# One load of r for a whole batch, six tokens to a partition, in a fused RWKV and token-mixing kernel

## The chip, the cores and the metric

The kernel runs on one core of one Trainium2 chip. The metric is the device time of one execution in microseconds (us); lower is better. The engines named below are TensorE (PE; PEld is its weight load), VectorE (DVE), ScalarE (ACT), GpSimd (POOL) and SyncE (SP), which here only issues DMAs.

## The reference

Two layers in sequence, for 4 batches, 8 heads, 768 tokens and 48 channels a head, all float32. The first is a linear attention with a state that decays per channel:

```python
for t in range(S):
    kt, vt, rt = (k[:, :, t], v[:, :, t], r[:, :, t])
    cur = np.einsum('bhd,bhe->bhde', u[None] * kt, vt)
    y[:, :, t] = np.einsum('bhd,bhde->bhe', rt, state + cur)
    state = w[None, :, :, None] * state + np.einsum('bhd,bhe->bhde', kt, vt)
```

Its output, with the heads side by side, is x (768 tokens by 384 channels for a batch). The second layer mixes tokens and channels:

```python
theta = x @ w_theta
zr, zi = x * np.cos(theta), x * np.sin(theta)
y = np.einsum('ts,bsd->btd', w_tok_r, zr) + np.einsum('ts,bsd->btd', w_tok_i, zi)
u = x + y
out = u + np.maximum(u @ w_ch, 0.0)
```

## The kernel before

**Tiling.** A batch's 768 tokens are six chunks of 128, worked on as three pairs of chunks; `g` counts the pairs over all batches (0 to 11). For a pair, `front` loads k, r and v, multiplies k and r by powers of w (`decay`, giving the bf16 tiles Kw and Rw), transposes both with TensorE (`flip`: one matmul against the identity for each block of 128 x 128, all into one PSUM bank, then one copy out by ACT or DVE, giving KT and RT), and makes the scores (KT against RT), which DVE multiplies with a mask into mAT. PD is the product of RT and KT for the diagonal term with u; `diag` and `yd` bring that to the output. `outer` makes a pair's contribution to the state, which F, T, N and the copies Sb and Sd carry from pair to pair in order. `states`, `outputs` and `bonus` add up the output of the pair in PSUM, and it is copied to x. Then x is transposed (xT), theta is a matmul, ACT takes cosine and sine of it (trig), and DVE makes z = x times trig. `mixing` multiplies z with the token weights WrT and WiT, which are themselves transposed once at the beginning from loads that GpSimd casts to bf16 (`cast`, `weights`). For an output chunk the mixing has three parts, one for each pair of z. Then comes the channel matmul with Wch, a maximum with zero, a sum and the store.

**Two layouts of tokens.** In the first seven pairs (`PAIRS`) k, v and r are loaded with two neighbouring tokens of a head on one partition, so that a run in memory is 2 x 48 floats, 384 bytes; r is loaded that way in all twelve pairs. In the others k and v have one token on a partition, 192 bytes. A transpose of a paired tile comes out with the even tokens in one block and the odd ones in the next; the copy out of PSUM puts them in order, by reading the two blocks in turn (the argument `paired` of `flip`).

**Powers.** `rpow` and `kpow` hold the powers of w for the two tokens on a partition; ACT makes them with one exponential for each of the two, from the logarithm of w and the column of `tok_f` that holds a token's distance from the middle of the pair.

**Buffers.** Sixteen load buffers (`Ls`, 128 x 768 float32, called ld in the profile) are given to the loads in turn. There are two Rw, four Kw, four RT and three KT, and eight PSUM banks.

**Order.** Every piece of work is a task in `Plan`. `ORDER` is one list of all tasks, written out beforehand; each engine runs its tasks in that order, and waits on semaphores for what a task reads or overwrites. `WAYS` says which engine does a task that several could do (copies out of PSUM, decay products, casts), `BANKS` gives the PSUM banks, `AFTER` adds waits between tasks that would otherwise run at the same time, and `IDLE` places filler matmuls on a tile of zeros (`unread`, line 293), whose result nobody reads. A load stands in SP's list, so a load that has to wait for its buffer also holds up what SP issues after it: other loads, transposes by DMA (line 510) and the stores.

**Lines.** 293 filler, 389 the logarithm, 399 the powers, 442 and 448 loads, 462 casting loads, 493 transposes, 503 and 504 their copies out by ACT and DVE, 554 and 556 decay products, 605 scores, 614 mAT, 621 PD, 638 and 643 the diagonal, 647 yd, 671 outer, 692 to 695 and 705 Sd, 719 F, 723 T, 726 and 727 N, 747 states, 760 outputs, 776 bonus, 784 and 786 x, 835 theta, 842 and 846 trig, 850 z, 901 mixing, 919 its sum, 929 the channel matmul, 956 to 964 the output.

Of the kernel before, what the change touches and what calls it, by code (L numbers as in the profile page):

```python
# [30 lines left out]
WARM, WARM_NS = (4, 6), (855, 1280)  # L31
NBANKS = 8
# [44 lines left out]
]  # L77
# [101 lines left out]
def kernel(  # L179
# [16 lines left out]
    C = 128  # L196
# [18 lines left out]
    def ring(n, shape, dt, nm):  # L215
        return [sb.tile(shape, dt, name=f"{nm}{i}") for i in range(n)]
# [81 lines left out]
    def setup():  # L298
# [93 lines left out]
        for i, (dst, nm, j, col) in enumerate((  # L392
# [3 lines left out]
            if dst is None:  # L396
                continue
# [623 lines left out]
```

## Time and profile before

| | |
|---|---|
| median of 3 runs | 136.62 us (136.30 to 137.31) |
| the profiled execution | 136.61 us, span 134.8 us |
| granted TensorE clock | 0.997 |
| PE busy | 127.9 us, 95% |
| DVE busy | 106.1 us, 79% |
| ACT busy | 81.0 us, 60% |
| POOL busy | 68.8 us, 51% |
| DMA | 25.47 MB in 67199 packets, 61801 of them under 512 bytes |

The span runs from the first instruction to the last; the time of an execution holds 1.8 us more around it. A line of a group names the source line, the engine, the operation and the tiles it writes and reads, then the shapes, the number of instructions, their busy time together, the mean of one in ns, and behind the second bar how long the engine was idle just before them and what ended that. A line of a timeline starts with the start and the duration in us. A line of the chain of work has start, duration, engine and line. A line of a table of stretches has the stretch, its length, and for each engine the busy us and the number of instructions; then the granted clock, the busy share of the DMA engines (above 1 where transfers overlap in the records) and GB/s.

### The profile page before, as it was taken

Reading aid. Unit: us, or ns where it says so; the run is one execution under the profiler, and the core shown is the slowest. Engines: PE = TensorE matmul, PEld = TensorE weight load, DVE = VectorE, ACT = ScalarE, POOL = GpSimd, SP = SyncE. Lnnn points to the kernel's source line nnn. Section 1 sums busy time; section 2 is a strip of 40 time slices with the busy share of each in tenths; the row PEclk is TensorE's granted clock in tenths of the full one; section 3 lists DMA queues with packets and bytes.
Section 4 is the critical chain, followed back from the end, with each engine's and each line's share of the span. In section 5 each row is a group of like instructions: output and inputs, shape, how many; then the busy total and the mean of one; then the engine's idle time right before and its main releaser. Section 6 shows DMA issues by size and latency. Waiting matters only on the chain.

```text
span 134.8 us, 4625 instructions
## 1 busy us (share of the span) xinstructions
PE 127.9 (95%) x1943; PEld 85.8 (64%) x1943; DVE 106.1 (79%) x201; ACT 81.0 (60%) x157; POOL 68.8 (51%) x76
## 2 busy tenths in 40 slices
PE   6999998899999999999999999899999999999970
PEld 1346666765776775876676776566667757667840
DVE  5099988687998999889798878799899997351370
ACT  3478696598968596684965153863731758900220
POOL 6003789295160456827326989664056955370220
PEclk9999999999999999999999999999999999999998
DMA  3999999999999955797999999979899950326344
GB/s 92 265 269 261 143 204 197 255 258 234 242 277 236 261 138 74 144 209 139 281 180 234 171 189 253 163 134 309 196 302 198 103 116 8 117 79 198 78 177 173
DMA packets 67199, 25.47 MB, mean 189 GB/s; under 512 B 61801, under 2 KB 67178, under 8 KB 67178
## 3 DMA queue, kind: packets, MB, share of 16 engines
q1 hardware_dynamic: 64744, 22.23, 76.3%
q0 software_dynamic: 2432, 2.95, 13.4%
q8 instruction: 15, 0.25, 0.8%
q14 instruction: 6, 0.05, 0.1%
q10 hardware_dynamic: 2, 0.00, 0.0%
HBM read 20.06 MB, written 4.72 MB: 184 GB/s over the span
## 4 chain that ended last, share of the span: by engine, by line
PE 78%; DVE 7%; DMA 5%; ACT 2%; POOL 2%; issue 2%; DVEq 0%; POOLq 0%; ACTq 0%
PE bank L901 31%; PE bank L493 11%; PE bank L835 8%; PE bank L929 7%; DMA uu_all<-uu_all 5%; PE bank L605 4%; PE bank L876 3%; PE bank L671 3%; PE bank L760 2%; PE bank L293 2%; DVE Rw L554 2%; PE bank L747 2%; PE bank L776 1%; PE bank L812 1%; PE bank L638 1%
## 5 line engine op out<-in xcount | busy, mean ns | idle before, releaser
L901 PE MATMUL bank<-z,WrT 128*128 128x384 bf16 x132 | 43.0, 326 | 0.0
L901 PE MATMUL bank<-z,WiT 128*128 128x384 bf16 x132 | 42.9, 326 | 0.0
L959 POOL TENSOR_TENSOR fin_all<-fin_all,uu_all 128x384 f32<-128x384 f32 x20 | 19.5, 992 | 22.7 <-ACT fin_all L956 8.7
L647 POOL TENSOR_TENSOR yd<-dg,vb 128x768 bf16<-128x768 f32 x10 | 14.7, 1471 | 11.8 <-DVE PD L621 5.1
L614 DVE TENSOR_TENSOR mAT<-bank,mask 128x512 bf16<-128x512 f32 x28 | 18.4, 682 | 0.3 <-PE bank L605 0.2
L901 PEld LDWEIGHTS <-WrT 128*128 128x128 bf16 x132 | 12.9, 98 | 7.7 <-issue 0.3
L956 ACT ACTIVATE fin_all<-bank 128x384 f32<-128x384 f32 x20 | 9.7, 494 | 12.9 <-issue 8.5
L901 PEld LDWEIGHTS <-WiT 128*128 128x128 bf16 x132 | 12.9, 98 | 7.1
L919 DVE TENSOR_TENSOR uu_all<-bank,x 128x384 bf16<-128x384 f32 x22 | 11.7, 553 | 5.3 <-PE bank L901 5.1
L842 ACT ACTIVATE trig<-bank,pi 128x384 f16<-128x384 f32 x24 | 13.4, 582 | 3.2 <-PE bank L835 3.2
L835 PE MATMUL bank<-Wth,xT 128*128 128x384 bf16 x72 | 14.3, 326 | 0.0
L850 DVE TENSOR_TENSOR z<-x,trig 128x1536 bf16<-128x1536 bf16 x12 | 11.4, 952 | 3.5 <-ACT trig L842 1.8
L846 ACT ACTIVATE trig<-bank 128x384 f16<-128x384 f32 x24 | 11.3, 490 | 4.5 <-PE bank L835 4.5
L929 PE MATMUL bank<-Wch,uu_all 128*128 128x384 bf16 x69 | 13.3, 326 | 0.4 <-DMA uu_all<-uu_all 0.4
L614 DVE TENSOR_TENSOR mAT<-bank,mask_c 128x512 bf16<-128x512 f32 x20 | 13.1, 682 | 0.0
L293 PE MATMUL bank<-zero 128*128 128x512 bf16 (+1 forms) x47 | 11.8, 377 | 1.3 <-DVE zero L300 1.3
L503 ACT ACTIVATE RT<-bank 128x1024 bf16<-128x1024 bf16 x10 | 10.2, 1022 | 4.2 <-PE bank L493 4.2
L554 POOL TENSOR_TENSOR Rw<-ld,rpow 128x768 bf16<-128x768 f32 x5 | 9.0, 1810 | 5.1 <-DVE z L850 4.4
L621 POOL TENSOR_TENSOR PD<-RT,KT 128x1024 bf16<-128x1024 bf16 x4 | 8.5, 2120 | 5.9 <-DVE RT L504 4.5
L503 ACT ACTIVATE KT<-bank 128x1024 bf16<-128x1024 bf16 x9 | 9.2, 1025 | 1.9 <-PE bank L493 1.8
L554 DVE TENSOR_TENSOR Kw<-ld,kpow 128x768 bf16<-128x768 f32 x7 | 6.7, 950 | 3.6 <-ACT kpow L399 3.6
L605 PE MATMUL bank<-RT,KT 64*64 64x128 bf16 (+1 forms) x304 | 8.8, 219 | 0.0
(122 smaller groups left out, 231.2 us busy)
## 6 DMA issues: line engine op xcount, KB each, us to landing
ld<-in_r_dram SPq DMA_DIRECT2D x12, 384.0 KB, 5.7
out_dram<-fin_all SPq DMA_DIRECT2D x11, 384.0 KB, 2.5
ld<-in_k_dram SPq DMA_DIRECT2D x7, 384.0 KB, 6.0
ld<-in_v_dram SPq DMA_DIRECT2D x7, 384.0 KB, 6.1
ld<-in_k_dram SPq DMA_DIRECT2D x10, 192.0 KB, 4.6
ld<-in_v_dram SPq DMA_DIRECT2D x10, 192.0 KB, 4.7
uu_all<-in_moe_w_tok_r_dram POOLq DMA_DIRECT2D x1, 384.0 KB, 5.3
fin_all<-in_moe_w_tok_i_dram POOLq DMA_DIRECT2D x1, 384.0 KB, 6.3
```

The costliest lines, as they stand in the source:

```text
L293: ins = [nc.tensor.matmul(bank_t[k][:, :wide * C].rearrange("p (a c) -> p a c", a=wide), zero, bc(zero, 1, wide), start=True, stop=True, s ...
L493: ins = [nc.tensor.matmul(bank16(tok)[:, i * C:(i + 1) * C], s, ident, is_transpose=True, start=(i == 0), stop=(i == n - 1)) for i, s in e ...
L503: P.add([act(n * C, lambda: nc.scalar.activation(dst, src(), Act.Copy)), dve(n * C, lambda: nc.vector.tensor_copy(dst, src()), 1.0 if pair ...
L554: return eng.tensor_mul(to.rearrange("p j h d -> p h j d")[:, :, :, :D], tokens(i), pw)
L605: ins.append(nc.tensor.matmul(to[:, hp * C:(hp + 1) * C], a, m, start=(hp == 0), stop=(hp == HP - 1), skip_group_check=True))
L614: mask01[:, j] if pairs else mask_c): nc.vector.tensor_mul(
L647: return eng.tensor_mul(yd.rearrange("p a b d -> p (a b) d"), wide(dg, D), vb.rearrange("p a b d -> p (a b) d"))
L835: ins = [nc.tensor.matmul(bank(th)[:, :HD], xT[:, t, dk, :], Wth[:, dk, :], start=(dk == 0), stop=(dk == ND - 1)) for dk in range(ND)]
L842: P.add(act(HD, lambda th=th, t=t, trig=trig: nc.scalar.activation(trig[:, t, 0], bank(th)[:, :HD], Act.Sin, bias=pi2), 144), use=[th], rd ...
L901: ins.append(nc.tensor.matmul(bank(tm)[:, :HD], (WrT, WiT)[ri][:, so, to * C:(to + 1) * C], z[:, so, ri], start=(part == 0 and i == 0), st ...
L929: ins = [nc.tensor.matmul(bank(tf)[:, :HD], uT[:, t, dk, :], Wch[:, dk, :], start=(dk == 0), stop=(dk == ND - 1)) for dk in range(ND)]
L959: P.add(pool(900, lambda t=t, un=un, fin=fin: nc.gpsimd.tensor_add(fin[:, t], fin[:, t], un[:, t])), rd=[("un", j, t)], wr=[("fin", j, t)] ...
```

## The change

r of a whole batch is loaded by one DMA: a partition gets six neighbouring tokens of each head, a run of 6 x 48 floats, 1152 bytes. It takes three neighbouring load buffers of the now twelve, which lie in one tile `ld_all`; where three don't fit before the end of the ring, the rest of it is skipped. The powers of r become `rpow6`, one exponential for each of the six tokens, with the distance of a token from the middle of its pair of chunks made by five small DVE operations (`tok6`). The decay product is still made in three parts, now two of the six tokens of each partition at a time, and every part needs the whole load. The transposes go by two heads: six blocks, one for each of the six tokens, in one bank, and the copy out puts the 768 tokens of those two heads in order; there are four such groups for a batch instead of three groups of eight blocks. RT is one tile for a batch (`RT6s`, two of them). k and v are loaded and transposed as before. `ORDER`, `WAYS`, `BANKS`, `AFTER` and `IDLE` are all written anew; `IDLE` asks for twenty fillers at six places where it asked for 37 at nineteen. On DVE, two of the three decay products and two of the four copies of the second batch's r now stand ahead of the first z.

```diff
+R6, R6_NS = (0, 1, 2, 3), 50
...
-    (4, 1, 1, 4), (72, 4, 1, 4), (72, 4, 1, 1), (74, 5, 1, 4),
-    (74, 5, 1, 1), (29, 7, 2, 1), (80, 1, 2, 4), (77, 4, 3, 4), (77, 4, 1, 1), (123, 2, 5, 4),
-    (123, 2, 3, 1), (84, 4, 2, 4), (84, 4, 3, 1), (120, 5, 2, 4), (120, 5, 3, 1), (50, 3, 1, 4),
-    (50, 3, 1, 1), (52, 3, 1, 4), (146, 4, 3, 1),
+    (4, 1, 1, 4), (6, 3, 10, 4), (127, 2, 3, 4), (127, 2, 1, 1), (98, 0, 2, 4), (101, 3, 3, 4),
...
-    NL, NR, NK, NV, NRT, NKT, NPD, NM, NSB, ND_ = 15 if KR_BY_DMA else 16, 2, 4, 6, 4, 3, 2, 5, 6, 3
+    NL, NK, NV, NKT, NPD, NM, NSB, ND_ = 12, 4, 6, 3, 2, 5, 6, 3
...
-    Ls = ring(NL, [C, 2 * HD], F32, "ld")
-    Rws = ring(NR, [C, 2, H, Dp], BF16, "Rw")
+    ld_all = sb.tile([C, NL * 2 * HD], F32, name="ld_all")
+    Ls = [ld_all[:, 2 * HD * i:2 * HD * (i + 1)] for i in range(NL)]
+    Rw6 = sb.tile([C, NCH, H, Dp], BF16, name="Rw6")
+    Rws = [Rw6[:, 2 * i:2 * i + 2] for i in range(NP)]
+    rpow6 = sb.tile([C, H, NCH, D], F32, name="rpow6")
...
-    RTs = ring(NRT, [C, 2 * HP * C], BF16, "RT")
+    RT6s = ring(2, [C, HP * S], BF16, "RT6")
...
+        def tok2_6():
+            a = nc.vector.tensor_copy(tok6[:, 0], tok6_i)
...
+            return a, nc.vector.tensor_tensor(tok6[:, 0], tok6[:, 0], tok6[:, 2], op=Alu.add)
...
+        for j in range(NCH) if R6 else ():
+            P.add((ACT, 510, False, lambda j=j: nc.scalar.activation(
+                rpow6[:, :, j, :], lw_f, Act.Exp, scale=tok6[:, 0, j:j + 1])),
...
     def load(src, b, pr, what, pairs):
-        i = nload[0] % NL
         nload[0] += 1
+        if what == "r" and b in R6:
+            if pr:
+                return None
+            if slot[0] % NL + NP > NL:
+                slot[0] += NL - slot[0] % NL
+            i = slot[0] % NL
+            slot[0] += NP
+            P.add(sp(lambda: nc.sync.dma_start(
+                out=ld_all[:, 2 * HD * i:2 * HD * (i + NP)].rearrange("p (h n) -> p h n", h=H),
+                in_=src[b].rearrange("h (p j) d -> p h (j d)", j=NCH))),
...
-            return a.rearrange("p (a j) t -> p a t j", j=2) if paired else a
+            return a.rearrange("p (a j) t -> p a t j", j=paired) if paired else a
...
+            if b in R6 and pr == 0:
+                t6 = ld_all[:, 2 * HD * ir:2 * HD * (ir + NP)].rearrange(
+                    "p (h j d) -> p h j d", h=H, j=NCH)
+                for m in range(NP):
+                    def decay6(eng, m=m, t6=t6):
+                        return eng.tensor_mul(
+                            Rws[m].rearrange("p j h d -> p h j d")[:, :, :, :D],
+                            t6[:, :, 2 * m:2 * m + 2, :], rpow6[:, :, 2 * m:2 * m + 2, :])
...
+                for hp in range(HP):
+                    flip(RT6[:, NCH * C * hp:NCH * C * (hp + 1)].rearrange("p (a t j) -> p a t j", a=1, j=NCH),
+                         [Rw6[:, j, 2 * hp:2 * hp + 2, :].rearrange("p h d -> p (h d)")
+                          for j in range(NCH)], ("TR", g, hp), pb,
+                         [("Rw", m) for m in range(NP)],
+                         [("RT", b % 2, m, hp) for m in range(NP)], paired=NCH)
```

More of the change, by code (lines that the diff above doesn't have):

```diff
@@ L229 @@
     tok_f = sb.tile([C, 9], F32, name="tok_f")
-    rpow = sb.tile([C, H, 2, D], F32, name="rpow")
     kpow = sb.tile([C, H, 2, D], F32, name="kpow")
@@ L238 @@
     uw = sb.tile([C, HP, 2], BF16, name="uw")
[L240 removed]
+    NL, NK, NV, NKT, NPD, NM, NSB, ND_ = 12, 4, 6, 3, 2, 5, 6, 3
     NSD = min(4, 2 * len(PAIRS))
[L242 to L243 removed]
+    ld_all = sb.tile([C, NL * 2 * HD], F32, name="ld_all")
[3 more added lines that the diff above has]
+    rpow6 = sb.tile([C, H, NCH, D], F32, name="rpow6")
+    tok6_i = sb.tile([C, NCH], mybir.dt.int32, name="tok6_i")
+    tok6 = sb.tile([C, 3, NCH], F32, name="tok6")
     Kws = ring(NK, [C, 2, H, Dp], BF16, "Kw")
     vbs = ring(NV, [C, 2 * HD], BF16, "vb")
[L246 removed]
+    RT6s = ring(2, [C, HP * S], BF16, "RT6")
+    rpow = RT6s[1][:, :4 * HD].bitcast(F32).rearrange("p (h j d) -> p h j d", h=H, j=2)
+    krpow = [("RT", 1, m, hp) for m in range(NP) for hp in range(HP)]
     KTs = ring(NKT, [C, 2 * HP * C], BF16, "KT")
@@ L385, in setup @@
               name="pads")
-        P.add(pool(260 * NR, lambda: pads(Rws)), wr=[("Rw", i) for i in range(NR)], prio=-202,
+        P.add(pool(260 * NP, lambda: pads(Rws)), wr=[("Rw", i) for i in range(NP)], prio=-202,
               name="pads")
@@ L395, in setup @@
                 (rpow_c, "rpow_c", 0, 7), (rpow_c, "rpow_c", 1, 8))):
-            if dst is None:
+            if dst is None or (nm == "rpow" and 0 in R6):
                 continue
@@ L400, in setup @@
                 to, lw_f, Act.Exp, scale=tok_f[:, col:col + 1])),
-                rd=["lw_f", "tok_f"], wr=[(nm, j), ("exp", i)],
+                rd=["lw_f", "tok_f"] + krpow * (nm == "rpow" and j),
+                wr=[(nm, j), ("exp", i)] + krpow * (nm == "rpow" and not j),
                 prio=-199 + 0.1 * i, name="pow")
+        for j in range(NCH) if R6 else ():
+            P.add((ACT, 510, False, lambda j=j: nc.scalar.activation(
+                rpow6[:, :, j, :], lw_f, Act.Exp, scale=tok6[:, 0, j:j + 1])),
+                rd=["lw_f", "tok6"], wr=[("rpow6", j), ("exp", 10 + j)],
+                prio=-197 + 0.1 * j, name="pow6")
         def wu_load():
@@ L424, in setup @@
         P.add((ACT, 1290, False, lambda: nc.scalar.preload_act_table_set("trig_and_small")),
-              rd=[("exp", i) for i in range(10) if KR_BY_DMA or i not in (6, 7)], wr=["sin"], prio=-195, name="sin set")
+              rd=[("exp", i) for i in range(16 if R6 else 10)
+                  if (KR_BY_DMA or i not in (6, 7)) and
+                  (0 not in R6 or i not in (2, 3))], wr=["sin"], prio=-195, name="sin set")
         def uw_fill():
@@ L433, in setup @@
         P.add((DVE, 300, False, uw_fill), use=["wu"], rd=["wup"], wr=["uw"], prio=-80, name="uw")
-    nload = [0]
+    nload, slot = [0], [0]
     def load(src, b, pr, what, pairs):
-        i = nload[0] % NL
         nload[0] += 1
+        if what == "r" and b in R6:
[8 more added lines that the diff above has]
+                in_=src[b].rearrange("h (p j) d -> p h (j d)", j=NCH))),
+                wr=[("L", i + m, c) for m in range(NP) for c in range(2)],
+                prio=-90 + 0.001 * nload[0], desc=(0, 64, R6_NS), name="load " + what,
+                kind="load")
+            return i
+        i = slot[0] % NL
+        slot[0] += 1
         rows = src[b, :, 2 * pr * C:(2 * pr + 2) * C, :]
@@ L576, in front @@
                      [Tw[:, j, 2 * hp:2 * hp + 2, :].rearrange("p h d -> p (h d)")
-                      for hp in range(HP) for j in range(2)], (nm, g), pb, [kT], [kTT],
-                     paired=two)
+                      for hp in range(HP) for j in range(2)], (nm, g), pb, [kT], kTT,
+                     paired=2 * two)
             flat_v, flat_l = vbs[g % NV], Ls[iv]
@@ L608, in scores @@
                     return ins[0], ins[-1]
-                P.add(pe(220, scores), rd=[kKT, kRT], acq=tk,
+                P.add(pe(220, scores), rd=[kKT] + kRT, acq=tk,
                       wr=[("mAT", mi, hi) for hi in range(2)] + [("scores", g, j)],
```

76 lines of the change are left out of this document (53 added, 23 removed), and 89 rows, old and new, of tables (AFTER, ORDER).

## The prediction

> **What bounds the kernel now.** The page comes first: its span and the busy shares. Then the table of stretches, once for all instructions and once for the filler matmuls of L293 alone, which multiply a zero tile for no result.
>
> ```profile
> span 134.8 us, 4625 instructions
> PE 127.9 (95%) x1943; PEld 85.8 (64%) x1943; DVE 106.1 (79%) x201; ACT 81.0 (60%) x157; POOL 68.8 (51%) x76
> ```
>
> ```profile
> core 0: us, PE busy (x) PEld busy (x) DVE busy (x) ACT busy (x) POOL busy (x), PEclk, DMA share, GB/s
> 8.00:20.00 12.00, 11.90 (x237) 7.87 (x238) 11.55 (x27) 9.60 (x17) 6.48 (x9) 1.00 1.16 215
> 20.00:30.95 10.95, 10.00 (x240) 7.32 (x238) 8.79 (x17) 8.26 (x20) 7.67 (x8) 1.00 1.10 236
> 30.95:80.00 49.05, 49.04 (x856) 34.63 (x857) 44.25 (x74) 34.20 (x67) 25.59 (x24) 1.00 1.00 200
> 80.00:86.00 6.00, 5.60 (x74) 3.65 (x75) 5.27 (x10) 3.19 (x7) 5.42 (x4) 1.00 1.20 198
> 86.00:129.33 43.33, 43.33 (x526) 29.84 (x525) 31.39 (x52) 21.33 (x46) 21.57 (x21) 1.00 0.69 152
> ```
>
> ```profile
> 8.00:20.00 12.00, 5.59 (x30) 2.27 (x31) 1.00 1.16 215
> 20.00:30.95 10.95, 1.15 (x6) 0.47 (x6) 1.00 1.10 236
> ```
>
> The span is one long run of TensorE with a loose beginning. From 30.95, where the first token-mixing matmul starts, to 129.33 PE is busy 49.04 + 5.60 + 43.33 = 97.97 of 98.38 us, with no filler. From 8.00 to 30.95 it is busy 21.90 us, of which 6.74 are filler: 15.16 us of work in 22.95, so 7.79 are lost. Since PE runs its list in order, the rule for any new order is: **the end moves by as much as the first mixing matmul moves, less the work that was pulled ahead of it**. What holds the beginning is in the timeline.
>
> ```profile
> 5.70 1.12 ACT L399 ACTIVATE kpow<-z,tok_f 128x384 f32<-128x384 f32 x2
> 6.73 1.10 ACT L399 ACTIVATE rpow<-z,tok_f 128x384 f32<-128x384 f32 x2
> 6.86 0.96 DVE L554 TENSOR_TENSOR Kw<-ld,kpow 128x768 bf16<-128x768 f32 x1 [3.57 <-ACT kpow L399]
> ...
> 9.69 0.84 DVE L374 MEMSET Sd<- 128x192 uint32 x4
> ...
> 17.01 2.48 DVE L614 TENSOR_TENSOR mAT<-bank,mask 128x512 bf16<-128x512 f32 x4
> ...
> 29.96 0.94 DVE L850 TENSOR_TENSOR z<-x,trig 128x1536 bf16<-128x1536 bf16 x1
> ```
>
> ```profile
> 6.86:29.96 23.10, 21.94 (x440) 14.69 (x438) 20.48 (x43) 17.84 (x34) 13.74 (x16) 1.00 1.13 226
> ```
>
> DVE's first decay product waits for the powers from ACT (two per 1.03 us), and from there to the first z it is busy 20.48 of 23.10 us, 89%. The beginning is DVE's list, not the loads: of the groups below, Rw waited 0.2 us for a load and Kw 3.6 for ACT.
>
> **The change, part by part.** Durations of DVE:
>
> ```profile
> L554 DVE TENSOR_TENSOR Rw<-ld,rpow 128x768 bf16<-128x768 f32 x7 | 7.3, 1050 | 0.3 <-DMA ld<-in_r_dram 0.2
> L554 DVE TENSOR_TENSOR Kw<-ld,kpow 128x768 bf16<-128x768 f32 x7 | 6.7, 950 | 3.6 <-ACT kpow L399 3.6
> L621 DVE TENSOR_TENSOR PD<-RT,KT 128x1024 bf16<-128x1024 bf16 x8 | 5.6, 695 | 0.6 <-ACT KT L503 0.5
> ...
> L723 DVE TENSOR_TENSOR T<-bank,F 128x192 f32<-128x192 f32 x8 | 2.8, 351 | 0.2
> L786 DVE CAST x<-bank 128x384 bf16<-128x384 f32 x5 | 2.8, 558 | 3.1 <-PE bank L776 3.0
> L504 DVE COPY RT<-bank 128x1024 bf16<-128x1024 bf16 x2 | 2.4, 1214 | 0.0
> ...
> L647 DVE TENSOR_TENSOR yd<-dg,vb 128x768 bf16<-128x768 f32 x2 | 1.9, 951 | 0.0
> ...
> L354 DVE TENSOR_SCALAR mask<-col_i,thr 128x128 bf16<-128x128 int32 x2 | 0.5, 284 | 0.0
> ...
> L431 DVE TENSOR_TENSOR uw<-bank,wup 64x4 bf16<-64x4 f32 x2 | 0.3, 162 | 0.0
> ...
> L695 DVE CAST Sd<-N 64x192 bf16<-64x192 f32 x1 | 0.2, 241 | 0.0
> ```
>
> *The load.* Four loads of r take the place of twelve, each three times as large.
>
> ```profile
> GB/s 92 265 269 261 143 204 197 255 258 234 242 277 236 261 138 74 144 209 139 281 180 234 171 189 253 163 134 309 196 302 198 103 116 8 117 79 198 78 177 173
> ...
> q1 hardware_dynamic: 64744, 22.23, 76.3%
> ...
> ld<-in_r_dram SPq DMA_DIRECT2D x12, 384.0 KB, 5.7
> ```
>
> The first r is 3 x 384 KB = 1.18 MB and first in SP's list; at 92 and 265 GB/s over the first two slices (3.37 us each) 1.20 MB have come by 6.74. It lands as its first product can start, and k, v behind it land before they are due; gain nothing, loss nothing. Bounds: a packet of q1 costs 0.763 x 134.8 x 16 / 64744 = 25.4 ns for 343 bytes on average. If a six-token packet of 1152 bytes cost no more, a batch would save 2048 packets, 2048 x 25.4 / 16 = 3.25 us; if it cost by bytes, nothing. The Trainium skill (DMA: Bandwidth & Descriptors, "Specifications") says that a transfer needs at least 512 bytes for line rate, which speaks for the larger packets; by that the loads end sooner, and the sum by it is the first rival's. No row here times 1152-byte loads.
>
> *Powers.* ACT makes six of r (rpow6) and then two of k where it made two and two. At 0.515 us each from 5.70 they end at 5.70 + 7 x 0.515 + 0.6 = 9.9. DVE's three r products fit between (6.86 to 9.85); its first k product starts at **9.95** instead of 6.86. The five small operations for tok6 lie before 6.86, where DVE is idle.
>
> *Transposes.* A batch's r takes four groups of six blocks instead of three of eight, 24 either way; all three Rw must be ready before the first. The copies out are 768 wide: on DVE 0.91 us (three quarters of 1.214, estimated from the RT row; bounds 0.55, were the gap between source elements free, and 1.21).
>
> *The new order on DVE*, from the first k product to the last x of batch 0, as its instruction list has it: two Kw and two Rw of the **next** batch, 4 x 0.95 = 3.80; twelve mAT at 2.48 / 4 = 0.62, 7.44; three PD, 2.10; two F, two T and two sums into Sd by the T row, 2.10; one KT copy in paired order, 1.21; one RT copy of the next batch, 0.91; two Sd casts, 0.48; the Sd blanks, 0.84; three masks, 0.84; wup and uw, 0.48; two x, 1.12; one yd, 0.95. Sum **22.27**, so 32.2 without a wait. I add 0.5 for waits: followed through the lists, the first mAT, F and T find their matmuls done, as ACT's four RT copies end before DVE gets through its KT copy. So 32.7. Bounds: no wait, 32.2; waits at the share of before (89% busy), 9.95 + 25.1 = 35.05. I take the value near the lower end, since the next batch's products stand in the list where before had to wait.
>
> *PE behind that x.* It runs these in order before the first mixing matmul: a transpose of x, Kw of the next batch, four of weights, two thetas and one scores.
>
> ```profile
> 24.53 0.35 PE bank L605 x16
> ...
> 25.32 0.49 PE bank L835 x3
> ...
> 30.95 0.81 PE bank L901 x4
> 31.77 0.34 PE bank L493 x6
> ...
> 41.79 0.45 PE bank L493 x8
> ```
>
> 5 x 0.34 + 0.45 + 2 x 0.49 + 0.35 = 3.48: the first mixing matmul starts at 32.7 + 3.5 = **36.2** instead of 30.95, 5.25 later. Pulled ahead of it, against before: two thetas 0.98, one x transpose 0.34, one of Kw 0.45, one scores 0.35, and r transposes 8 x 0.34 - 3 x 0.45 = 1.37, together **3.5**. So the end moves by 5.25 - 3.5 = **+1.75**. DVE's list ahead of the mixing contains more because two of the next batch's r products and copies went there; they are prepaid, but PE cannot be late at 30.95 and early later, for behind that point it has nothing to shed except 0.4 us in 80 to 86.
>
> *Filler* costs nothing where it is: it fills time in which PE waits anyway. *Twelve load buffers*: a batch's r takes three neighbours and is asked for after all of them are read. SP's list is held by that twice: the second r behind the first k product (about 11), needed by DVE at about 24, and the third behind a product on POOL at about 31, needed after 45. Both have over ten us against a landing of 5.7; cost nothing. Without that cover each us late would be one us of DVE's list.
>
> Sum against the profiled execution: 136.61 (span 134.80 and 1.81 around it) + 1.75 = 138.4. The median of the runs shown is 136.62, the same.
>
> **The rivals.** *Loads set the beginning, and it ends sooner (faster).* For it: DMA is full in the early slices. Against it: the 0.2 us. Were it so, the first r saves 3.25 us, the beginning keeps its 7.79 lost us otherwise, and the time is 136.6 - 3.25 = 133.4. To be faster by 1% the mixing has to begin before 30.95 + 3.5 - 1.37 = 33.1.
>
> *The delay is mostly hidden (no change).* DVE runs without a wait and the 0.4 us at 80 to 86 vanish because that transposing DMA finds emptier queues: 35.7 - 34.45 - 0.4 = +0.85, 137.5. It turns into my forecast with half a us of waits.
>
> *TensorE falls back to its slow clock (slower still).*
>
> ```profile
> 5.08 2.74 PE L293 MATMUL bank<-zero 128*128 128x512 bf16 x6
> ...
> 8.40 0.43 PE L293 MATMUL bank<-zero 128*128 128x512 bf16 x2
> ```
>
> A filler takes 2.74 / 6 = 0.457 us at the beginning and 0.215 later: matmuls speed up after 6.5 us of activity (1.26 to 7.8). The new order has no filler after its second group of scores (about 17), while PE is lightly loaded up to 30. If it slowed for 6.5 us at 70% load, 4.6 us of work would take 4.6 longer, 1.9 of it in gaps: +2.7, 141.1. Against it: the longest gap I find is about 1.2 us. The Trainium skill (TensorE: Matmul & The Clock Gate, Part 1) sets the fall at an idle window of about 3.4 us; by that rule it would not happen, which keeps its chance low.
>
> That r doesn't land by 6.86 is a miss of the same kind as the forecast: each us late is one us on 9.95.
>
> **How the numbers follow.** Forecast (DVE's longer list, 137.9 to 140.7): 0.55. Clock: 0.07. No change: 0.27. Faster: 0.11. One per cent, 1.37 us, is about what a measurement of this kernel tells from no change. Faster 0.11, within 1% 0.27, slower 0.55 + 0.07 = 0.62. The range runs from 136.0, in the no-change case, to 140.9, just above DVE waiting at its old share (38.55 - 34.45 = +4.1, 140.7); outside lie the faster case and most of the clock's.
>
> **What would show it.** Right: the first k product at about 10; DVE over 95% busy from there to the x of the third pair at 32 to 33; the first mixing matmul at 36; PE unbroken behind it. The step on the list is wrong if mixing starts before 34 or DVE idles over 2 us; the step on the loads if Rw's first product starts after 7.5 or anything waits for ld before 30; the no-recovery step if PE's work behind the first mixing matmul takes less than 94.9 us (98.4 - 3.5) up to the last transposes, or shows new holes. A fresh hole behind 40 us from SP's longer waits would make the time worse than my range.

## The result, and the profile after

The changed kernel takes **141.81 us** (median of four runs, 140.77 to 144.09) against 136.66 for the kernel before on the same chip: a ratio of 1.036, with a 95% interval of 1.028 to 1.044. It is slower, as forecast, but by +5.2 us and not by +1.75; the time lies above the range. The ratio compares the executions within 1.5% of the fastest of their kernel, which leaves out the one of 144.09.

The profiled execution of the changed kernel took 142.65 us. From its page, the span, the busy times and the granted clock:

```profile
span 140.9 us, 4606 instructions
PE 130.5 (93%) x1926; PEld 86.1 (61%) x1926; DVE 110.8 (79%) x214; ACT 76.5 (54%) x151; POOL 68.5 (49%) x84
...
PEclk9999999999999999999995999999999999999997
```

One slice of the clock row, the 22nd (74.0 to 77.5 us), is at 5. First the beginning. From the timeline of the changed kernel (start, length, engine, line):

```profile
7.08 2.76 DVE L615 TENSOR_TENSOR Rw<-ld_all,rpow 128x768 bf16<-128x768 f32 x3 [1.98 <-DMA ld_all<-in_r_dram]
9.89 0.96 DVE L607 TENSOR_TENSOR Kw<-ld_all,kpow 128x768 bf16<-128x768 f32 x1
...
31.55 0.55 DVE L863 CAST x<-bank 128x384 bf16<-128x384 f32 x1
...
35.82 0.33 PE L978 MATMUL bank<-z,WrT 128*128 128x384 bf16 x1
```

The first k product starts at 9.89, the third x ends at 32.10 and the first mixing matmul starts at 35.82, where 9.95, 32.2 to 32.7 and 36.2 were forecast. Behind it things went otherwise. The table of stretches of the changed kernel (length, then busy us of PE, PEld, DVE, ACT, POOL, the granted clock, the DMA share, GB/s):

```profile
core 0: us, PE busy (x) PEld busy (x) DVE busy (x) ACT busy (x) POOL busy (x), PEclk, DMA share, GB/s
8.00:20.00 12.00, 10.85 (x200) 6.96 (x199) 11.02 (x25) 9.06 (x18) 4.38 (x6) 1.00 1.21 284
20.00:35.82 15.82, 14.53 (x330) 10.72 (x316) 15.52 (x27) 13.98 (x25) 11.23 (x13) 1.00 0.86 157
35.82:70.00 34.18, 33.61 (x617) 23.18 (x615) 31.76 (x56) 21.62 (x42) 18.43 (x19) 1.00 0.98 208
70.00:76.00 6.00, 3.87 (x27) 1.99 (x26) 3.53 (x5) 2.39 (x6) 1.25 (x2) 0.86 0.98 236
76.00:79.00 3.00, 3.00 (x15) 1.57 (x14) 2.31 (x3) 0.00 (x0) 0.54 (x1) 0.70 1.36 211
79.00:136.44 57.44, 57.44 (x749) 39.48 (x748) 41.71 (x75) 24.94 (x54) 30.22 (x32) 1.00 0.69 133
```

From 70 to 76 TensorE is busy 3.87 of 6 us, and until 79 its clock is down. What it waited for stands in its waits (engine, line, releaser, total, times, longest) and in SP's timeline and the chain:

```profile
PE bank L912 <- DMA xT<-x: 2.1, 1, 2.1
...
PE bank L748 <- ACT vb L658: 0.4, 1, 0.4
```

```profile
64.12 0.58 SPq L475 DMA_DIRECT2D ld_all<-in_r_dram  x1
64.80 1.26 SPq L554 DMA_TRANSPOSE xT<-x  x1
```

```profile
29.65 9.76 DMA ld_all<-in_v_dram
...
64.80 8.20 DMA xT<-x
```

The transposing DMA of x, issued 0.7 us behind the fourth r load, took 8.20 us to land (2.9 in the median of its kind), so the thetas wait 2.13 us at 71. Not all of that need be r's bytes. The trace records the landing in sixteen parts: fifteen of xT's had come by 71.48 and the last came at 73.01, while the instruction queues have a packet of 8 KB at 69.54 and one of 16 KB at 70.80 (0.31 and 1.12 us long). Whether these held up that last part was not tested. In the kernel with filler in the hole (experiment 8) all sixteen came within 0.15 us of each other, 8.38 us after the issue, so r can hold xT that long without them.

A v load that left SP only at 29.65, because a half load of k ahead of it stood waiting for the second batch's r products, makes the 0.43 us wait at 40. Behind the hole at 71 the mixing matmuls come half as fast:

```profile
74.20 0.36 PE L978 MATMUL bank<-z,WiT 128*128 128x384 bf16 x1
...
76.28 0.53 PE L978 MATMUL bank<-z,WrT 128*128 128x384 bf16 x1
```

Ten of them between 74.36 and 77.56 stand 0.32 us apart and not 0.163: 3.20 - 1.63 = 1.6 us lost.

**The sum of the profiled executions** (142.65 - 136.61 = 6.04):

| term | us | from |
|---|---|---|
| first mixing matmul later | +4.87 | 35.82 - 30.95 |
| work of TensorE pulled ahead of it | -3.45 | groups behind the first mixing matmul, below |
| hole at 71, for xT | +2.13 | waits |
| clock at 74 to 78 | +1.6 | timeline |
| wait for vb at 40 | +0.43 | waits |
| rest | +0.5 | |

The second term comes from the groups of matmuls behind the first mixing one, before and after: r transposes 72 and 48, thetas 60 and 54, k transposes 72 and 64, transposes that read z 24 and 12, those that read x 24 and 30, scores 128 and 112; 24 x 0.056 + 6 x 0.163 + 8 x 0.056 + 12 x 0.056 - 6 x 0.056 + 16 x 0.022 = 3.45. (The token weights pass through tiles called z and x on their way, at other times in the two kernels; the rows for z and x together, 0.34, are one transpose of x itself.) The beginning is thus worth +1.4. The other executions fit: those at a full clock took 140.8 and 141.0, those with a granted clock of 0.976 and 0.982 took 141.7 to 142.7, and the one at 0.964 took 144.1.

### The profile page after: what moved, and what is told of

Read it like the earlier page. It is cut to its first block, busy times and chain, and to the rows that moved or that the text cites. A ratio compares the mean times of both kernels' runs of the same rounds, so it can differ in the third digit from the quotient of the medians.

```text
span 140.9 us, 4606 instructions
## 1 busy us (share of the span) xinstructions
PE 130.5 (93%) x1926; PEld 86.1 (61%) x1926; DVE 110.8 (79%) x214; ACT 76.5 (54%) x151; POOL 68.5 (49%) x84
## 4 chain that ended last, share of the span: by engine, by line
PE 67%; DMA 13%; DVE 7%; POOL 5%; issue 2%; ACT 2%; SPq 0%; DVEq 0%; ACTq 0%; POOLq 0%
PE bank L978 27%; PE bank L537 7%; DMA ld_all<-in_v_dram 7%; PE bank L1006 6%; DMA xT<-x 6%; PE bank L298 6%; PE bank L912 5%; PE bank L682 3%; PE bank L953 3%; POOL yd L724 2%; PE bank L748 2%; PE bank L889 2%; PE bank L837 1%; DVE mAT L691 1%; PE bank L316 1%
## 5 line engine op out<-in xcount | busy, mean ns | idle before, releaser
L978 PE MATMUL bank<-z,WrT 128*128 128x384 bf16 x132 | 44.1, 335 | 0.0
L978 PE MATMUL bank<-z,WiT 128*128 128x384 bf16 x132 | 44.0, 334 | 0.0
L1036 POOL TENSOR_TENSOR fin_all<-fin_all,uu_all 128x384 f32<-128x384 f32 x20 | 17.9, 912 | 24.0 <-ACT fin_all L1033 16.0
L724 POOL TENSOR_TENSOR yd<-dg,vb 128x768 bf16<-128x768 f32 x8 | 11.8, 1473 | 7.2 <-ACT dg L720 5.9
L298 PE MATMUL bank<-zero 128*128 128x512 bf16 (+1 forms) x30 | 10.4, 502 | 1.3 <-DVE zero L305 1.3
L912 PEld LDWEIGHTS <-xT 128*128 128x128 bf16 x72 | 6.7, 98 | 6.6 <-DMA xT<-x 2.5
L547 ACT ACTIVATE RT<-bank 128x768 bf16<-128x768 bf16 x12 | 9.4, 810 | 2.1 <-PE bank L537 2.1
L607 POOL TENSOR_TENSOR Kw<-ld_all,kpow 128x768 bf16<-128x768 f32 x2 | 3.6, 1808 | 13.7 <-DVE mask L374 12.6
L720 ACT ACTIVATE dg<-bank 128x16 f32<-128x16 f32 x12 | 2.2, 185 | 14.6 <-PE bank L715 10.8
L615 DVE TENSOR_TENSOR Rw<-ld_all,rpow 128x768 bf16<-128x768 f32 x9 | 8.5, 987 | 2.0 <-DMA ld_all<-in_r_dram 2.0
```

Of the source, the lines that this page charges most:

```text
L298: ins = [nc.tensor.matmul(bank_t[k][:, :wide * C].rearrange("p (a c) -> p a c", a=wide), zero, bc(zero, 1, wide), start=True, stop=True, s ...
L547: P.add([act(n * C, lambda: nc.scalar.activation(dst, src(), Act.Copy)), dve(n * C, lambda: nc.vector.tensor_copy(dst, src()), 1.0 if pair ...
L724: return eng.tensor_mul(yd.rearrange("p a b d -> p (a b) d"), wide(dg, D), vb.rearrange("p a b d -> p (a b) d"))
L912: ins = [nc.tensor.matmul(bank(th)[:, :HD], xT[:, t, dk, :], Wth[:, dk, :], start=(dk == 0), stop=(dk == ND - 1)) for dk in range(ND)]
L978: ins.append(nc.tensor.matmul(bank(tm)[:, :HD], (WrT, WiT)[ri][:, so, to * C:(to + 1) * C], z[:, so, ri], start=(part == 0 and i == 0), st ...
L1036: P.add(pool(900, lambda t=t, un=un, fin=fin: nc.gpsimd.tensor_add(fin[:, t], fin[:, t], un[:, t])), rd=[("un", j, t)], wr=[("fin", j, t)] ...
```

## The experiments

All times are medians of four runs (six for the spread kernel with filler) with the ratio to the kernel before on the same chip; the kernel before took 136.8 to 137.2 in these jobs. Task 537 is the fourth r load, 312 the transposing DMA of x that was late; 540 and 542 are the two r products on VectorE that read that load.

**1. The load somewhere else in SP's list.** Ahead of the stretch in which SP was idle, and behind the late transposing DMA:

```diff
 ORDER (load earlier)
-    380, 292, 325, 381, 382, 376,
+    380, 292, 325, 381, 382, 537, 376,
...
-    364, 537, 421,
+    364, 421,
```

> Only SP's list is changed: the fourth load of r is issued right after the buffers are free (about 56 us, where the DMA engines are nearly idle) instead of one place before the transposing DMA of x (64.8). Queue theory (1.18 MB ahead in SP's queue made that transpose land after 8.2 us instead of about 2.9): theta no longer waits, the 2.1 us hole of PE before 73 and the slow clock behind it are gone, time 141.8 - 2.1 - up to 1.7 = 138.0 to 139.5. Crowding theory (all DMA traffic of this stretch makes the transpose slow, wherever r stands): the hole keeps more than 1.2 us and the time stays at 141 to 142.

```diff
 ORDER (load behind the transposing DMA)
-    364, 537, 421, 362, 280, 312, 365,
+    364, 421, 362, 280, 312, 537, 365,
```

> The fourth load of r is issued one place later, right behind the transposing DMA of x instead of right ahead of it: the same bytes in the same stretch. Queue theory: the transpose lands after about 3 us, no hole at 73, the clock stays full; r lands about 1.3 us later, which DVE waits for at 71 (it does that product at once now), PE has other work; 138.0 to 139.8. Crowding theory: the transpose still takes 6 us or more, hole over 1.2 us, 141 to 142.

Measured: 143.72 us (1.047, 1.034 to 1.059) and 141.28 us (1.028, 1.020 to 1.037). In both the wait for xT is gone, and another has come. TensorE's waits, load earlier and then load behind the turn:

```profile
PE bank L1006 <- DMA uu_all<-uu_all: 1.6, 1, 1.6
...
PE bank L537 <- DVE Kw L609: 1.2, 1, 1.2
```

```profile
PE bank L978 <- DVE z L927: 1.7, 1, 1.7
```

In the first, r left SP at 57.71, and what SP issued next is late: a transposing DMA of uu, and a half load of k that took 7.56 us, for whose product TensorE waits. (That profile has one more wait, 1.8 us at 47 to 49 for token weights. It lies ahead of the moved load, so the move didn't make it.) In the second, the z stood behind the r products in VectorE's list, and they waited 2.56 us for the load. So I moved the products too.

**2. The products later as well.** On top of the load behind the turn, 540 and 542 stand behind the z and the mixing sums, and the extra wait of a state sum for 542 is left out.

```diff
 ORDER
-    313, 540, 316,
+    313, 316,
...
-    420, 542, 317,
+    420, 317,
...
-    526, 405, 433, 406, 468, 462,
+    526, 540, 405, 433, 406, 468, 542, 462,
 AFTER
-    (542, 402),
```

> The fourth r load stands behind the transposing DMA of x in SP's list, as in the run with the load alone behind it, and the two r products on VectorE that wait for that load stand some 8 us later in VectorE's list, behind the z and the sums of the mixing; the extra wait of a state sum on GpSimd for the second of them is left out. Theory (1.18 MB in one piece holds up whatever waits for it or stands behind it in the queue): neither xT nor z waits for r, the 2.1 us hole at 71 and the 1.7 us one at 75 are both gone, the clock stays full there, and the time is 2 to 3.5 us below the changed kernel's 141.8, about 138.5 to 140. Rival (the steady part is short of VectorE time, the waits were only where it showed): holes open elsewhere between 75 and 95 us, and the time stays at 141 or above.

Measured: 142.69 us (139.79 to 143.15). One execution of the four, 139.79, lies in the forecast range; the other three took 142.3 to 143.2, too far apart for a ratio. The profiled one, 142.27, shows the rival's picture: a hole of the same size a little later. The releaser was a load again. From VectorE's timeline and TensorE's waits:

```profile
75.32 0.96 DVE L610 TENSOR_TENSOR Kw<-ld_all,kpow_c 128x768 bf16<-128x768 f32 x1 [1.38 <-DMA ld_all<-in_k_dram]
```

```profile
PE bank L979 <- DVE mAT L692: 1.7, 1, 1.7
```

The k load behind r came late, its product held up VectorE's list, and the masks behind it TensorE.

**3. r behind k too, and a v load earlier.**

```diff
 ORDER (on the kernel of 2)
-    312, 537, 365,
+    312, 365,
...
-    334, 454, 346,
+    334, 454, 537, 346,
```

540 stands behind 427 and 542 behind 490; in the second kernel also 199, a load of v, ahead of 417, the half load of k that holds SP's list.

> The fourth r load stands in SP's list behind the transposing DMA of x and also behind the two half loads of k that follow it; its two products on VectorE stand some 12 us later than in the changed kernel, and the extra wait of a state sum for one of them is left out. In the run with r behind the transposing DMA alone and the products later, k landed at 75.3 behind r and a hole of 1.7 us opened at 80. Theory (what stands behind the 1.18 MB in SP's list is late by its 4 to 5 us, whatever it is): with nothing urgent behind r, the k product starts at about 73, no hole of over 1 us opens between 64 and 90, TensorE is busy over 9.5 of 10 us in 80 to 90, and the time at full clock is 138.5 to 139.5 (the changed kernel's 140.9 less its 2.1). Rival (VectorE's list is too full there): a hole opens behind the r products at 86 to 95 and the time stays at 140 or above.

> The edit with r behind the transposing DMA and behind k, and besides one v load of 384 KB stands ahead of the half load of k that holds SP's list from 14.3 to 28.6 us, so that it is issued at about 14.3 and not at 29.7. Theory (SP's list held by the r product costs the 0.43 us in which TensorE waits for vb at 39.9): that wait is gone, time 0.4 us below its twin without this edit. Rival (the load takes bandwidth from the first weights, which TensorE needs at 25.8): the thetas start later than 25.8 and the time is the same or up to 1 us above the twin's.

Measured: 144.46 us (1.047, 1.039 to 1.055) and 145.49 us (1.062, 1.055 to 1.069): the forecast of 138.5 to 139.5 fails. Now v, behind r, is what lands late (the chain), and TensorE waits for it (waits):

```profile
71.61 7.29 DMA ld_all<-in_v_dram
```

```profile
PE bank L1007 <- DVE uu_all L997: 1.7, 1, 1.7
PE bank L749 <- POOL vb L663: 1.6, 1, 1.6
```

The other wait, for the sums, is of a new kind: moved to 82, the r products ran beside GpSimd's work and took 2.3 to 2.6 us instead of 0.95 (last section). The earlier v load took the 0.4 us wait at 40 away, but in that execution the clock was at 0.5 from 21 to 27; nothing was gained.

**4. Another queue.** Is the queue at fault, or the DMA engines behind all queues?

```diff
-            P.add(sp(lambda: nc.sync.dma_start(
+            P.add((ACT if b == 3 else SP, 560, False, lambda: (nc.scalar if b == 3 else nc.sync).dma_start(
```

> The fourth r load is issued by ScalarE at the same place in the order instead of by SP; all else as in the changed kernel. If the transposing DMA is late because it stands behind r in the same queue, it lands in about 3 to 4 us, the 2.1 us hole at 71 is gone, and the time comes to about 139 to 140.5. If it is late because r takes the bandwidth of the DMA engines, whichever queue it is in, it still takes 5 to 8 us and the hole and the time stay.

Measured: 144.49 us (1.056, 1.050 to 1.062). ScalarE issued r at 62.59. SP was then issuing a transposing DMA of uu, from 61.72 to 64.09, and that DMA landed 7.81 us after its start (the timelines of SP and ScalarE, then the chain). TensorE waited for it (waits):

```profile
60.45 3.64 SPq L554 DMA_TRANSPOSE uu_all<-uu_all  x2
```

```profile
62.59 0.40 ACTq L475 DMA_DIRECT2D ld_all<-in_r_dram  x1
```

```profile
61.72 7.81 DMA uu_all<-uu_all
```

```profile
PE bank L1006 <- DMA uu_all<-uu_all: 3.0, 1, 3.0
```

From 64.3 to 67.0 the trace has packets of ScalarE's queue alone, 772 of them. So it isn't the order within a queue: the large load held up a transposing DMA of another queue, which SP had begun to issue before r and finished after it.

**5. Three DMAs for one.**

```diff
+            def three():
+                to = ld_all[:, 2 * HD * i:2 * HD * (i + NP)].rearrange("p (h q n) -> p h q n", h=H, q=NP)
+                rows = src[b].rearrange("h (p q j) d -> p h q (j d)", q=NP, j=2)
+                ins = [nc.sync.dma_start(out=to[:, :, q], in_=rows[:, :, q]) for q in range(NP)]
```

> Each of the four loads of r goes as three DMAs of 384-byte runs (two of the six tokens of a partition each) in place of one with 1152-byte runs; same bytes, same place in the list, same tiles. By bytes (the theory, from the busy time of the queue: 1623 against 1645 engine-us for 8192 packets fewer): the first r lands within 0.5 us of before, the queue's busy time rises by under 3%, and the time stays within 1 us of 141.8. By packets (the rival: a packet has a price of its own): the first r lands 1.5 to 3.3 us later and the beginning and the hole at 71 us grow, 143 to 146. If pieces let the transposing DMA between, its wait of 8.2 us gets shorter.

Measured: 141.34 us (1.033, 1.025 to 1.042), the same as the changed kernel. The hole for xT is there (1.7 us). The busiest queue and the first r products of this kernel:

```profile
q1 hardware_dynamic: 64744, 22.23, 77.7%
```

```profile
7.51 2.70 DVE L619 TENSOR_TENSOR Rw<-ld_all,rpow 128x768 bf16<-128x768 f32 x3 [2.42 <-DMA ld_all<-in_r_dram]
```

77.7% of 139.6 us on 16 engines is 1735 engine-us, against 72.0% of 140.9, 1623, with 8320 packets fewer. Large packets are worth 7% of the queue's time, between my two bounds, and 0.43 us at the first r; in the time, nothing that shows. That the load is *one* DMA matters little either way. That its bytes come *together* is what is left.

**6. The bytes themselves.** First most of them are taken away (two of the eight heads are loaded, the rest of the last batch's r is left out), then all are kept but spread. The second needs a thirteenth buffer; a fourth buffer of Kw makes room.

```diff
+            n = 2 if b == 3 else H
             P.add(sp(lambda: nc.sync.dma_start(
-                out=ld_all[:, 2 * HD * i:2 * HD * (i + NP)].rearrange("p (h n) -> p h n", h=H),
-                in_=src[b].rearrange("h (p j) d -> p h (j d)", j=NCH))),
+                out=ld_all[:, 2 * HD * i:2 * HD * (i + NP)].rearrange("p (h n) -> p h n", h=H)[:, :n],
+                in_=src[b, :n].rearrange("h (p j) d -> p h (j d)", j=NCH))),
```

> As the changed kernel, but the fourth r load brings two of the eight heads (288 of 1152 KB), at the same place in the same queue; the other heads' rows hold what was there, so part of r of the last batch is left out. All instructions of the engines are the same. Theory (the 1.18 MB at that point takes the DMA engines for 4 to 5 us, and what is due then is late): the transposing DMA of x lands in about 3 to 4 us instead of 8.2, the 2.1 us hole at 71 is gone, k and v behind it land in time, no new hole over 1 us opens between 64 and 95, and at a full clock the time is 138.3 to 139.3, the changed kernel's 140.9 less 2.1 and what the later loads cost. Rival (the holes come from the order of VectorE and the waits of SP's list, not from the bytes): holes of 1 to 2 us stay between 64 and 95 and the time is 140 or above.

```diff
-    NL, NK, NV, NKT, NPD, NM, NSB, ND_ = 12, 4, 6, 3, 2, 5, 6, 3
+    NL, NK, NV, NKT, NPD, NM, NSB, ND_ = 13, 3, 6, 3, 2, 5, 6, 3
...
+            for a, z, ms in ((0, 5, (0, 1)), (5, H, (1, 2))) if b == 3 else ((0, H, (0, 1, 2)),):
+                P.add(sp(lambda a=a, z=z: nc.sync.dma_start(
+                    out=to[:, a:z],
+                    in_=src[b, a:z].rearrange("h (p j) d -> p h (j d)", j=NCH))),
```

In SP's list the five heads stand behind 536, a half load of k, and the three behind 312.

> The whole of r, in the changed kernel's layout, but the fourth r load is cut in two by heads and spread in time: five heads (720 KB) as soon as their two buffers are free, in the stretch from 51 to 58 in which SP is idle and the DMA engines are half idle, and three heads (432 KB) behind the transposing DMA of x. For that there are 13 load buffers instead of 12 (and 3 buffers of Kw instead of 4, to make room). Theory (it is the bytes at one point that cost): no transposing DMA waits, r is complete by about 70, VectorE does not wait for it, and at a full clock the time is 138.5 to 139.7. Rival (any new place only moves the hole): 140.5 or above, as in the five other places tried.

Measured: 139.47 us (1.018, 1.013 to 1.024) with a quarter of the load, 140.36 us (1.022, 1.016 to 1.029) with it spread; their profiled executions took 138.62 and 138.70. The changed kernel's ratio was 1.036 (1.028 to 1.044): the interval of the first lies below it, that of the second just meets it. With a quarter of the load xT lands in 4.0 us and not 8.2, and no wait of TensorE behind the first mixing matmul is above 0.2 us. Of the spread kernel, SP's two r loads, all of TensorE's waits behind its first mixing matmul, and two stretches:

```profile
52.35 0.82 SPq L478 DMA_DIRECT2D ld_all<-in_r_dram  x1
...
64.78 0.57 SPq L478 DMA_DIRECT2D ld_all<-in_r_dram  x1
```

```profile
engine line waited for: us in total, times, longest us
PE bank L685 <- DVE T L803: 0.2, 1, 0.2
```

```profile
35.84:70.00 34.16, 34.02 (x624) 23.48 (x622) 32.30 (x57) 21.80 (x43) 18.39 (x20) 1.00 1.05 229
70.00:133.00 63.00, 62.75 (x778) 42.24 (x775) 48.80 (x81) 27.59 (x60) 31.93 (x34) 1.00 0.76 145
```

TensorE is busy 96.8 of 97.2 us from 35.84 to 133. All of r is loaded, in the changed layout, through the changed tiles, and the holes are gone: it was the 1.18 MB at one point in time. What is left of this execution is 138.70 - 136.61 = +2.1. The first mixing matmul, at 35.84, makes +1.4 of that as before; the other 0.7 has no single place. The other three executions of the spread kernel took 140.4 to 140.7, two of them at a clock of 0.97 and one at a full clock; they have no profile, so what they lost is not shown.

**7. The beginning: VectorE's list.** Two masks and the blanks go into the time in which VectorE waits for the first r; in a second kernel with experiment 2 as well.

```diff
 ORDER
-    6, 13, 23,
+    6, 13, 16, 15, 20, 23,
...
-    35, 16, 79,
+    35, 79,
...
-    128, 15, 98,
+    128, 98,
...
-    101, 20, 102,
+    101, 102,
```

> Two masks and the blanking of the state tiles (0.28 + 0.48 + 0.84 = 1.6 us on VectorE) stand in the 1.98 us in which VectorE waits for the first r, not behind its first products. Nothing else is changed. Theory (VectorE's list sets the first mixing matmul): the third x comes 1.6 us earlier and the first mixing matmul starts at about 34.2 instead of 35.8; with no work of TensorE pulled ahead the end comes up to 1.6 us earlier, about 140.2. Rival (TensorE's chain through its transposes and thetas, or the weights' landing, sets it): first mixing at 35.3 to 35.8, no change in time.

> Both edits together: r behind the transposing DMA with its products later, and VectorE's idle stretch used. If the two losses are separate terms of the sum, the gains add: 3 to 5 us below the changed kernel, 137 to 139, about the kernel before. If they share one cause, it is no better than the better of the two.

Measured: 142.51 us (1.040, 1.034 to 1.047) and 143.36 us (1.040, 1.031 to 1.049). Neither gained. Up to the clock's fall the first kernel can be read: its F sum at 20.57 stands at 20.71 in the changed kernel, so 1.6 us off VectorE's list gave 0.14. Freed, VectorE waited 1.36 us for the k transposes: TensorE's transposes and ScalarE's copies run abreast of the list. Then the clock fell (stretch, and first mixing matmul):

```profile
21.00:24.00 3.00, 2.96 (x72) 1.93 (x66) 2.04 (x4) 1.96 (x3) 2.86 (x5) 0.50 0.10 18
```

With the clock at 0.50 from 21 to 27 the first mixing matmul came at 37.23, not 35.82. How far VectorE's list alone sets the beginning stays open.

**8. The clock and the filler.** Ten fillers in the hole at 71; the late fillers taken out of the kernel *before*; fillers in the beginning of the spread kernel.

```diff
 IDLE, changed kernel (task, bank, count, width)
+    (503, 2, 10, 4),
 IDLE, kernel before
-    (120, 5, 2, 4), (120, 5, 3, 1), (50, 3, 1, 4), (50, 3, 1, 1), (52, 3, 1, 4), (146, 4, 3, 1),
 IDLE, spread kernel
+    (109, 2, 1, 4), (137, 6, 2, 4), (140, 0, 1, 4), (159, 1, 2, 4),
```

> Ten fillers of 512 columns (2.15 us) are put in front of the theta matmul that waits for the transposed x; nothing else. Clock theory: the hole stays (PE gets the data at 73 as before), but the matmuls behind it keep 0.16 us each instead of 0.32, the mean granted clock is 0.995 or more in every run, and the median falls to that of the runs of the changed kernel that had the full clock: 140.8 to 141.0. If the slow matmuls behind the hole come from something other than the idle time (weights or z arriving slowly), the clock share and 141.8 stay.

> The kernel before, without its filler matmuls from 16.5 us on (14 of 47: five at 16.75, two at 20.02, one at 21.84, three at 29.14 and what lies between). My prediction costed filler at nothing. By that, the time is unchanged at 136.7 and the granted clock stays full. By the clock theory (filler keeps the granted clock up where TensorE waits for the first chain), the clock falls to about 0.5 for some 6 us between 20 and 30 in some or all executions, as it did in five profiles of the changed order, and those take 1 to 2 us longer: mean granted clock 0.97 to 0.99, 137.5 to 139.

> The kernel with the fourth r load spread, and besides six filler matmuls of 0.21 us at four places between 18 and 28 us where TensorE waits (1.96 of 3 us busy in 18 to 21). Its twin's profiled execution had no hole behind 36 us and took 138.7 at a granted clock of 0.995, but three other executions took 140.4 to 140.7, two of them at a clock of 0.97. Theory (what is left above 138.7 is a cold stretch of the clock in the beginning, as five profiles of the changed order showed at 21 to 27 us): with filler the clock stays at 0.99 or above in all executions and the median comes to 138.5 to 139.2. Rival (the clock falls for another reason, or filler cannot fill the waits since the bank that it writes is the one waited for): clocks of 0.97 stay and the median is 140 or above, or the first mixing matmul starts over 0.4 us later than 35.84.

Measured: 141.67 us (1.033, 1.025 to 1.041); 136.47 us (0.997, 0.992 to 1.002); 139.80 us (1.021, 1.017 to 1.025). Filling the hole kept the clock up behind it, but in the profiled execution it fell in the beginning instead, at 21 to 27. The two executions at a full clock took 141.2 and 142.2, no less than the changed kernel's 140.8 and 141.0, so the filler gained nothing that shows. The kernel before doesn't need its late filler (eleven matmuls, not the 14 that the expectation counts): clocks of 0.993 to 0.997, the same time. The spread kernel with filler kept 0.994 or more in all six executions, where two of its twin's four were at 0.97. The stretch from 18 to 21 in the kernel before without late filler, and in the spread kernel with filler:

```profile
18.00:21.00 3.00, 2.48 (x62) 1.86 (x62) 2.63 (x6) 2.81 (x5) 2.87 (x4) 1.00 1.23 205
```

```profile
18.00:21.00 3.00, 2.44 (x44) 1.59 (x47) 2.97 (x8) 2.75 (x8) 2.94 (x6) 1.00 1.06 206
```

TensorE is busy 2.4 to 2.5 of 3 us there and the clock holds; in the changed kernel it is 1.96, and the clock holds in some executions and not in others. But the filler moved the first mixing matmul to 36.80, and at a full clock the six executions still range from 138.7 to 141.3; in the longest, 1.0 us of TensorE's waits is again for a k load. That spread is not explained.

**9. The load that holds SP's list.** The half load of k that waits for the second batch's r products stands later.

```diff
 ORDER
-    181, 417, 207,
+    181, 207,
...
-    306, 418,
+    306, 417, 418,
```

> One half of a k load of a late pair, which stands early in SP's list and waits there for the second batch's r products (SP idle from 14.3 to 28.6), is moved to the place of its other half; the loads behind it go 10 us earlier. List theory (this wait made v of the fourth pair land at 39.4, so that the outer product at 39.8 waited 0.5 us on PE, 1.0 on DVE): the first loads after 14 us are issued before 20, the hole at 40 is gone, 0.4 to 1.0 us faster, 140.8 to 141.4, the hole at 73 unchanged. If v's late landing cost nothing further on, 141.8.

Measured: 143.01 us (1.043, 1.034 to 1.052). The loads go out early, and the beginning gets worse: the first weights (Wth) land after 7.1 us and not 5.3, and the first mixing matmul stands at 37.81. TensorE's wait in the middle of a group of scores at 25 has no releaser in the profile, and the clock falls behind it, at 26.6. The hole for xT is gone; in its place TensorE waits 1.3 us at 66 for a k product.

```profile
PE bank L682 <- issue: 1.5, 1, 1.5
```

So SP's idle stretch from 14 to 28 us isn't a loss by itself: with it, the weights land earlier.

## Why the prediction was right in part and wrong in size

- **What bounds the kernel, and the rule of the first mixing matmul**: right. Pulled-ahead work 3.45 against 3.5, the beginning +1.4 against +1.75. Where nothing waits behind it (the spread kernel's profiled execution), the time comes out at +2.1.
- **The first load**: r products at 7.08 against 6.86, no loss to speak of. Packets cost between "by bytes" and "by count" (experiment 5). The faster rival fell: the loads don't set the beginning, and larger packets gave nothing. The rule of the Trainium skill that it named (DMA: Bandwidth & Descriptors, "Specifications") points the right way, 1623 engine-us and not 1735, but the queue was not what bound there.
- **Powers, transposes, VectorE's list**: the times are right, 9.89 and 32.10. VectorE is busy 20.98 of the 22.21 us between, 94% and not over 95%: its waits were 1.2 us where I had 0.5, and its work was 1.3 us less. As a cause the list was too simple: TensorE's transposes bind within 0.14 us of it (experiment 7).
- **The step that failed: "Twelve load buffers: ... cost nothing."** I priced the large load by its own readers, for the second and the third r, and never followed the fourth. The price is paid by others: transposing DMAs beside 1.18 MB landed 4.4 and 5.3 us later than the median of their kind, half loads of k some 3 us later (7.3 against 4.4 and 4.7 with a quarter of r), and at 64 us it was xT that TensorE waited for (+2.1, and +1.6 by the clock's fall behind it). I also had SP's list held only by r's own waits; a half load of k held it from 14.3 to 28.6, which made the v load late that TensorE waited for at 40 (+0.4). My "what would show it" named a fresh hole behind 40 us as the thing that would break the range, but no rival carried it, and the range was built from the beginning alone.
- **"PE unbroken behind it"** fell with that step. That nothing is regained there was right.
- **Filler costs nothing**: right for the kernel before (experiment 8). **The clock rival** was right in mechanism and far too unlikely at 0.07: the profiled execution fell to half speed after the hole (1.6 us), and in eight of the fifteen profiles of the changed order the clock fell at 21 to 27 us, where I had thought it unlikely since no gap is long enough. In the three where it stayed down for 6.8 us (experiments 3 and 7) the first mixing matmul came at 37.2 to 37.5, 1.4 to 1.7 us later, against my 2.7; in the five with 3.4 us it came at 35.3 to 36.2, about where it came without a fall (35.7 to 35.9).
- **No change** fell; its terms (no wait of VectorE, a gain at 80 to 86) didn't come.

## What to carry to other kernels

Price a load not only by when its own reader needs it, but by what else is on the DMA engines in the next 5 us, on every queue: a transposing DMA or a small load that TensorE waits for pays for a large one beside it. Merging loads merges their bytes in time; here a stretch with idle DMA engines ahead was worth more than fewer packets. And when a step moves filler, look at TensorE's busy share over 3 us, not at its longest gap.

## What the runs showed of the hardware that I had not expected

**A large load delays a transposing DMA on another queue, even one whose issue began before it.** SP took from 61.72 to 64.09 to issue the DMA, ScalarE issued r at 62.59, and the DMA landed after 7.81 us instead of 3.4, the median of its kind in that kernel (experiment 4).

**The clock falls without a long gap.** With TensorE busy 1.96 of 3 us and no gap above 0.4 us the granted clock went to 0.5 in some executions; after single gaps of 2.13 us (the changed kernel) and 3.0 us (experiment 4) it fell too, after gaps of 1.7 and 1.8 us (experiment 1) it did not. After one of 1.5 us (experiment 9), in a stretch with 1.46 of 3 us busy, it did. The Trainium skill (TensorE: Matmul & The Clock Gate, Part 1) gives an idle window of about 3.4 us as the condition; here shorter gaps did it.

**VectorE's product beside GpSimd's takes more than twice as long.** In the kernel of experiment 3 with r behind k, from the timelines of VectorE and GpSimd:

```profile
82.43 2.31 DVE L616 TENSOR_TENSOR Rw<-ld_all,rpow 128x768 bf16<-128x768 f32 x1
```

```profile
82.12 1.81 POOL L610 TENSOR_TENSOR Kw<-ld_all,kpow_c 128x768 bf16<-128x768 f32 x1 [2.35 <-DVE yd L725]
```

GpSimd's ended at 83.93; VectorE's ended 0.8 us later, close to its usual 0.95 from there. The Trainium skill (SBUF — State Buffer, "Summary: rules for kernel authors") says that of a VectorE operation with two SBUF inputs and a GpSimd operation that reads SBUF the second waits until the first is done; these rows agree.
